# Attention and a gated feed-forward in one kernel: the constant of unseen keys from products on TensorE in place of pieces of ScalarE, and new ranks for the planner

## The chip, the core and the metric

The kernel runs on one core of a Trainium2 chip. The metric is device time in microseconds (us) of one execution. A core has five engines that run their own instruction queues beside each other and wait for one another by semaphores: TensorE (PE, products; PEld is its loading of weights), VectorE (DVE), ScalarE (ACT), GpSimd (POOL) and SyncE (SP, whose queue issues nearly all DMAs of this kernel). TensorE multiplies a stationary operand (up to 128 x 128) with a moving one and adds up in PSUM; the other engines read PSUM and work in SBUF.

## The reference

Block-causal attention (8 batches, 8 heads, 576 positions, 64 per head, blocks of 64), then a gated feed-forward on the 4608 rows of 512 that come out of it. The feed-forward's weights are 64-bit floats.

```python
scores = (1/sqrt(D)) * q @ k.T
mask   = (pos[:, None] // 64) >= (pos[None, :] // 64)
scores = where(mask, scores, -1e9)
attn   = exp(scores - max(scores)); attn /= sum(attn) + 1e-9
x      = (attn @ v) laid out as 4608 x 512
out    = (silu(x @ w_gate) * (x @ w_val)) @ w_out
```

## The kernel before

**Stages.** There is one program of some 7900 products, with no loop on the chip. Attention takes a batch's heads two at a time; the two heads sit in the two halves of 64 partitions (`own(x)`, x = 0 or 1), and their products stand in pairs. Keys are the partitions of the scores (chunks of 128, c = 0 to 4), queries the columns; a chunk needs only queries from c x 128 on. The first two batches (`early`) are cut into queries 0 to 255 and 256 to 575. Per pair of heads and stretch: transposes of q and k on PE (L410), ACT copies them out (L418, tile `parts`), scores on PE in plain float32 (L436, into the PSUM tiles `at` or `po`), ACT brings them to SBUF (L454, tile `sc`), DVE takes the maximum over chunks (L700, tile `mx`) and GpSimd over partitions (L704), DVE subtracts (L728), ACT takes the exponential (L732), and PE multiplies with the values and, in batch 0, with `ones` for the sums (L772). Batches 2 to 7 split q and k into high and low parts and take another path (`split_scores`, `row_scores`), which the change doesn't touch.

**The mask.** Only in a diagonal chunk, the one whose first query is c x 128, does the mask cut: its first 64 queries don't see its last 64 keys. So in the first 64 columns of such a chunk, partitions 64 to 127 need -1e9. Before, ACT adds it as a bias per partition (`unseen`: 0 in the upper half, -1e9 in the lower) in an operation of its own, after the plain copy: `hide` (L459, on 2 x 64 columns of one chunk), `hide_there` (L477, in PSUM itself, for batch 0's first 256 queries, whose scores stay in PSUM) and the second half of `first_max` (L468, beside a plain copy L467).

**Feed-forward.** 18 tiles of 256 rows. Per tile, six steps of two pieces of 128 hidden units: up products in reduced-width float32, three per 128 x 256 (high x high, high x low, low x high, L1095 to L1097, into two PSUM tiles `gv`), ACT's tanh (L1128), DVE's two gates (L1131, which also sets the gate's `gv` free, and L1136), ACT's high part (L1141), DVE's low part (L1144, `hhl`), and down products (L1186 to L1188, 128 x 512). Tiles 0 and 1 run in the first phase, their steps mixed in the order that `MIXED` gives.

**Weights.** 36 pieces of 512 KB are loaded into five raw buffers (tile `wo`) by SP (L939). Each is turned from 64-bit words into a high and a low part: ACT L954 and L958, DVE L963 and L968, ACT L973 (high) and DVE L976 (low). After L976 the raw buffer takes the next load.

**What sets the order.** Every piece of work is a `Task` with an engine, an estimated cost and a rank. `in_order` runs a model of the five engines while the kernel is built, gives an engine that is free the ready task of the lowest rank, and writes the tasks out in that order; nothing is decided on the chip. Ranks come from tables at the top: `PIECES` (weights, 12 x 3), `AHEAD` (their loads), `FIRST` (the two early batches, by stretch and pair of heads), `SIDE` (the feed-forward of tiles 0 and 1), `LEAD` and `EAGER` (later batches: rank 10 + b - LEAD), `spare` (how long an engine waits for a task of a better rank).

Of the kernel before, what the change touches and what calls it, by code (L numbers as in the profile page):

```python
# [18 lines left out]
def kernel(  # L19
# [17 lines left out]
    nc = tc.nc  # L37
# [15 lines left out]
    LEAD, EAGER = 1.69, 0.3  # L53
# [5 lines left out]
    MIXED = (0, 0, 1, 1, 0, 1, 0, 0, 1, 1, 0, 1)  # L59
# [3 lines left out]
    AHEAD = {(0, 1): 2.01, (0, 2): 2.07, (1, 0): 2.03, (1, 1): 2.5, (1, 2): 2.5}  # L63
    LATER = 0.6

    PIECES = [
        (2.46, 1.85, 2.03),
        (4.86, 5.95, 3.63),
        (4.60, 2.52, 1.48),
        (3.87, 3.06, 5.35),  # L70
        (1.93, 3.59, 2.41),
        (5.14, 6.91, 5.83),
        (3.58, 2.93, 2.93),
        (0.08, 1.36, 0.92),
        (-2.10, -5.86, -4.34),
        (-7.48, -5.87, -3.82),
        (-7.64, -9.14, -8.44),
        (-12.11, -9.50, -10.88),
    ]

    SIDE = (2.98, 4.19)
# [4 lines left out]
        0: [(0, 256, (-4.21, 2.41, 2.06, 2.12)), (256, 576, (-2.91, -2.07, -6.62, -4.11))],  # L86
        1: [(0, 256, (4.02, 3.94, 4.16, 3.63)), (256, 576, (-2.93, 1.90, 2.56, 4.50))],
# [97 lines left out]
    ones = const.tile([P, D], F32, name="ones")  # L185
# [4 lines left out]
    nc.vector.memset(unseen[BLK:P], HIDDEN)  # L190
    seen = const.tile([P, 1], F32, name="seen")
# [149 lines left out]
    def attention(R, b, h, a, e, early, bufs, lane):  # L341
# [4 lines left out]
        Q = R - (0.1 if early else EAGER)  # L346
# [30 lines left out]
        def plain_scores():  # L377
# [49 lines left out]
            for visit in visits:  # L427
                both = [Buf("at", also=banks) for _ in visit]

                def products(visit=visit, both=both):  # L430
                    for parts, ps in zip(visit, both):
                        o = 0
                        for c, qs, w in parts:
                            for x in range(2):
# [5 lines left out]
                                    start=True,  # L440
                                    stop=True,
# [3 lines left out]
                ws = [w for parts in visit for _, _, w in parts]  # L445
                pr = add("PE", pair_us(*ws), Q, products, ready, [*both, prt, sc], mode="rows")
                for parts, ps in zip(visit, both):
                    gw = sum(w for _, _, w in parts)
                    mixed = [(c, sum(w for _, _, w in parts[:i])) for i, (c, qs, _) in enumerate(parts) if qs == c * P]
# [6 lines left out]
                    def hide(mixed=mixed, ps=ps):  # L456

                        for c, o in mixed:
                            nc.scalar.activation(  # L459
                                sc[0][:, :, place[c] : place[c] + BLK],  # L460
                                ps[0][:, :, o : o + BLK],
                                AF.Identity,
                                bias=unseen,
                            )

                    def first_max(ps=ps):
                        nc.scalar.copy(mx[0][:, :, L + BLK : L + P], ps[0][:, :, BLK:P])  # L467
                        nc.scalar.activation(  # L468
                            mx[0][:, :, L : L + BLK], ps[0][:, :, 0:BLK], AF.Identity, bias=unseen
                        )  # L470

                    if whole:
                        stays.append(ps)

                        def hide_there(ps=ps):
                            x = ps[0].rearrange("p x (n w) -> p x n w", w=2 * P)[:, :, :, 0:BLK]
                            nc.scalar.activation(x, x, AF.Identity, bias=unseen)  # L477

                        def max_there(ps=ps):
                            nc.scalar.copy(mx[0][:, :, L : L + W], ps[0][:, :, 0:W])  # L480

                        t = add("ACT", act_us(4 * BLK) + 0.1, Q, hide_there, [pr], [ps])
                        t = add("ACT", act_us(2 * W), Q, max_there, [t], [ps, mx])
# [4 lines left out]
                    if mixed:  # L488
                        t = add("ACT", 0.245 * len(mixed), Q, hide, [t], [ps, sc])
                    if parts[0][:2] == (0, 0):  # L490
                        t = add("ACT", 0.46, Q, first_max, [t], [ps, mx])
# [791 lines left out]
    def in_order():  # L1283
# [14 lines left out]
        now = queue = 0.0  # L1298
        mode, last = "", None

        spare = {"PE": 2.12, "DVE": 0.32, "ACT": 0.75, "POOL": 0.0, "SP": 0.0}

        def place(t, by):

# [104 lines left out]
```

## Time and profile before

| | us |
|---|---|
| median of 3 runs | 1179.26 (1177.92 to 1181.79) |
| the profiled execution | 1177.14 |
| its span, first to last instruction | 1175.3 |
| PE busy from 0 to 200 us | 178.37 |
| DVE and ACT busy from 0 to 200 us | 167.18 and 158.44 |
| PE busy from 200 us to the end (975.3 us) | 970.65 |
| mean granted PE clock of the span | 0.994 |

Lines of the profile that the prediction reads are shown there. A group of a listing reads: line, engine, operation, output tile<-input tiles, shapes, count, then busy us and the mean ns of one, then the idle time of the engine just before such instructions and who ended it. In the trace a plain float32 product is two records. "gv L1095" in the waits and the chain stands for the tile that is written and the line that writes it.

### The profile page before, as it was taken

The numbers are of one execution on the slowest core, as the hardware profiler recorded it, in microseconds if no ns is written. First come the engines' busy times: TensorE is split into PE (matmuls) and PEld (weight loads), VectorE is DVE, ScalarE is ACT, GpSimd is POOL, SyncE is SP. The second block draws the span as 40 slices with busy tenths as digits, with TensorE's granted clock in tenths as the row PEclk, the third lists the DMA queues.
The fourth block names the chain that finished last, engine by engine and source line by source line (L and its number), as shares of the span: only waits on it lengthen the run. The fifth ranks groups of instructions, "written<-read, shape, count | busy, mean of one in ns | idle before, by whom it ended". The sixth has DMA issues, their size and how long they took to land.

```text
span 1175.3 us, 21803 instructions
## 1 busy us (share of the span) xinstructions
PE 1149.0 (98%) x8512; PEld 1026.9 (87%) x8512; DVE 754.4 (64%) x1226; ACT 625.0 (53%) x1122; POOL 323.7 (28%) x139
## 2 busy tenths in 40 slices
PE   6889999999999999999999999999999999999998
PEld 4568778898898989998999899899989899999997
DVE  5988988575887668768585867686857423323222
ACT  6889877546573837474656565656555212112111
POOL 3222100144535251335233433343324200000000
PEclk9899999999999999999999999999999999999999
DMA  8758756766554756755665565656553536453442
GB/s 213 200 150 217 197 187 227 209 177 166 170 145 139 198 165 167 218 148 158 177 173 153 155 175 146 191 157 173 151 182 125 160 136 190 145 168 135 144 132 102
DMA packets 266983, 197.40 MB, mean 168 GB/s; under 512 B 195264, under 2 KB 231376, under 8 KB 266880
## 3 DMA queue, kind: packets, MB, share of 16 engines
q1 hardware_dynamic: 264304, 195.29, 57.0%
q8 instruction: 67, 1.10, 0.4%
q10 hardware_dynamic: 2576, 0.72, 0.3%
q14 instruction: 36, 0.29, 0.1%
HBM read 171.57 MB, written 24.38 MB: 167 GB/s over the span
## 4 chain that ended last, share of the span: by engine, by line
PE 84%; DVE 6%; ACT 5%; DMA 2%; issue 1%; POOL 1%; SPq 1%; DVEq 0%; ACTq 0%; POOLq 0%
PE gv L1095 16%; PE gv L1097 15%; PE gv L1096 15%; PE po L1186 7%; PE po L1187 7%; PE po L1188 7%; PE at L772 7%; PE at L562 5%; DVE mx L700 1%; DMA wo<-in_moe_w_out_dram 1%; DVE sc L728 1%; PE po L772 1%; PE at L436 1%; ACT sc L732 1%; PE at L646 1%
## 5 line engine op out<-in xcount | busy, mean ns | idle before, releaser
L704 POOL PARTITION_ALL_REDUCE mx<-mx x80 | 142.9, 1833 | 400.4 <-DVE mx L700 126.3
L1095 PE MATMUL gv<-xhl,v_all 128*128 128x256 f32 x864 | 242.3, 280 | 0.8 <-DVE t L1131 0.7
L1097 PE MATMUL gv<-xhl,v_all 128*128 128x256 f32 x864 | 239.7, 277 | 0.2 <-DVE v_all L976 0.2
L1096 PE MATMUL gv<-xhl,v_all 128*128 128x256 f32 x864 | 239.5, 277 | 0.0
L823 POOL PARTITION_ALL_REDUCE mx<-mx x48 | 178.4, 3764 | 195.7 <-DVE mx L700 167.5
L1131 DVE SCALAR_TENSOR_TENSOR t<-t,gv 128x512 f32<-128x512 f32 x108 | 74.0, 685 | 190.4 <-ACT t L1128 190.2
L1095 PEld LDWEIGHTS gv<-xhl,v_all 128*128 128x128 f32 x864 | 162.1, 188 | 5.1 <-issue 2.5
L1096 PEld LDWEIGHTS gv<-xhl,v_all 128*128 128x128 f32 x864 | 162.3, 188 | 0.6
L1097 PEld LDWEIGHTS gv<-xhl,v_all 128*128 128x128 f32 x864 | 162.2, 188 | 0.4 <-DVE v_all L976 0.4
L1128 ACT ACTIVATE t<-gv 128x512 f32<-128x512 f32 x108 | 64.7, 599 | 173.4 <-PE gv L1097 173.3
L1186 PE MATMUL po<-wo,hhl 128*128 128x512 f32 x372 | 147.4, 396 | 0.2 <-ACT ob L1213 0.2
L1187 PE MATMUL po<-wo,hhl 128*128 128x512 f32 x372 | 145.7, 392 | 0.0
L1188 PE MATMUL po<-wo,hhl 128*128 128x512 f32 x372 | 145.1, 390 | 0.2 <-DVE hhl L1144 0.2
L1141 ACT CAST hhl<-t 128x512 fp32r<-128x512 f32 x108 | 67.1, 621 | 130.3 <-DVE t L1136 128.0
L732 ACT ACTIVATE sc<-sc 128x1024 f32<-128x1024 f32 (+3 forms) x104 | 105.9, 1031 | 52.2 <-DVE sc L728 51.5
L1136 DVE SCALAR_TENSOR_TENSOR t<-t,gv 128x512 f32<-128x512 f32 x108 | 73.8, 684 | 90.1 <-PE gv L1097 89.4
L728 DVE TENSOR_TENSOR sc<-sc,mx 128x640 f32<-128x640 f32 (+6 forms) x168 | 122.1, 766 | 13.9 <-POOL mx L704 13.8
L1095 PE MATMUL gv<-xhl,g_even 128*128 128x256 f32 x432 | 123.5, 286 | 0.0
L1097 PE MATMUL gv<-xhl,g_even 128*128 128x256 f32 x432 | 122.2, 283 | 0.0
L1096 PE MATMUL gv<-xhl,g_even 128*128 128x256 f32 x432 | 122.1, 283 | 0.0
L1095 PE MATMUL gv<-xhl,g_odd 128*128 128x256 f32 x432 | 120.8, 280 | 0.0
L1144 DVE TENSOR_TENSOR hhl<-t,hhl 128x512 fp32r<-128x512 f32 x108 | 91.2, 845 | 45.3 <-ACT hhl L1141 44.8
(172 smaller groups left out, 2445.4 us busy)
## 6 DMA issues: line engine op xcount, KB each, us to landing
wo<-wo_d SPq DMA_DIRECT2D x200, 512.0 KB
out_dram<-ob SPq DMA_DIRECT2D x35, 256.0 KB
v<-in_v_dram SPq DMA_DIRECT2D x64, 128.0 KB
xt<-x_d SPq DMA_DIRECT2D x64, 128.0 KB
rt<-r_d SPq DMA_DIRECT2D x128, 64.0 KB
qk<-in_q_dram SPq DMA_DIRECT2D x112, 72.0 KB
qk<-in_k_dram SPq DMA_DIRECT2D x104, 72.0 KB
x_d<-xu SPq DMA_DIRECT2D x24, 288.0 KB
```

What stands on the lines that cost most here:

```text
L704: nc.gpsimd.partition_all_reduce(m, m, channels=P, reduce_op=bass_isa.ReduceOp.max)
L728: nc.vector.tensor_tensor(piece(c), scores_of(c), m, ALU.subtract)
L732: nc.scalar.activation(x, x, AF.Exp)
L772: nc.tensor.matmul(ps[0][own(x), 1 - i if sums else i, q0 - s0 : s1 - s0], lhsT=ones if sums else vt[0][:, 2 * lane + c, own(x)], rhs=sc[0 ...
L823: nc.gpsimd.partition_all_reduce(m, m, channels=P, reduce_op=bass_isa.ReduceOp.add)
L1095: nc.tensor.matmul(o, lhsT=hi[:, d], rhs=xhi[:, 0:w], start=first, stop=False)
L1096: nc.tensor.matmul(o, lhsT=hi[:, d], rhs=xlo[:, 0:w], start=False, stop=False)
L1097: nc.tensor.matmul(o, lhsT=lo[:, d], rhs=xhi[:, 0:w], start=False, stop=last)
L1144: nc.vector.tensor_tensor(hh[1][:, 0:n], t[0][:, 0:n], hh[0][:, 0:n].bitcast(F32), ALU.subtract)
L1186: nc.tensor.matmul(po, lhsT=hi, rhs=whi, start=i + y == 0, stop=False)
L1187: nc.tensor.matmul(po, lhsT=hi, rhs=wlo, start=False, stop=False)
L1188: nc.tensor.matmul(po, lhsT=lo, rhs=whi, start=False, stop=i + y == NFC - 1)
```

## The change

The constant is added by PE, inside the scores' accumulation. A new tile `shade` has 64 columns of 0 and 64 of 1; a new column `hidden` is -1e9 in rows 0 and 64 and 0 elsewhere. After the scores of a diagonal chunk, one product for each head, stationary `shade` (64 rows x 128), moving `hidden` repeated over 64 columns, is added to the first 64 columns: 0 for the chunk's first 64 keys and -1e9 for the others. `hide`, `hide_there` and the second operation of `first_max` go; `first_max` becomes one plain copy. `ones` is now the second half of `shade`. The planner's tables get other numbers, `MIXED` swaps two steps, and early batches' first tasks (scores' evacuation, maxima) get the rank R - 1 in place of R - 0.1.

```diff
-    LEAD, EAGER = 1.69, 0.3
+    LEAD, EAGER = 1.32587, 0.3
-    MIXED = (0, 0, 1, 1, 0, 1, 0, 0, 1, 1, 0, 1)
+    MIXED = (0, 0, 1, 0, 1, 1, 0, 0, 1, 1, 0, 1)
...
-    ones = const.tile([P, D], F32, name="ones")
+    shade = const.tile([P, 2 * BLK], F32, name="shade")
+    nc.vector.memset(shade[:, 0:BLK], 0.0)
+    ones = shade[:, BLK : BLK + D]
     nc.vector.memset(ones, 1.0)
...
+    hidden = const.tile([P, 1], F32, name="hidden")
+    nc.vector.memset(hidden, 0.0)
+    for x in range(2):
+        nc.vector.memset(hidden[x * D : x * D + 1], HIDDEN)
...
-        Q = R - (0.1 if early else EAGER)
+        Q = R - (1 if early else EAGER)
...
                                     start=True,
-                                    stop=True,
+                                    stop=qs > c * P,
                                 )
+                            for x in range(2) if qs == c * P else ():
+                                nc.tensor.matmul(
+                                    ps[0][:, x, o : o + BLK],
+                                    lhsT=shade[own(x), :],
+                                    rhs=hidden[own(x), :].to_broadcast([D, BLK]),
+                                    start=False,
+                                    stop=True,
+                                )
...
-                    def hide(mixed=mixed, ps=ps):
-                        for c, o in mixed:
-                            nc.scalar.activation(
-                                sc[0][:, :, place[c] : place[c] + BLK],
-                                ps[0][:, :, o : o + BLK],
-                                AF.Identity,
-                                bias=unseen,
-                            )
                     def first_max(ps=ps):
-                        nc.scalar.copy(mx[0][:, :, L + BLK : L + P], ps[0][:, :, BLK:P])
-                        nc.scalar.activation(
-                            mx[0][:, :, L : L + BLK], ps[0][:, :, 0:BLK], AF.Identity, bias=unseen
-                        )
+                        nc.scalar.copy(mx[0][:, :, L : L + P], ps[0][:, :, 0:P])
...
-                        def hide_there(ps=ps):
-                            x = ps[0].rearrange("p x (n w) -> p x n w", w=2 * P)[:, :, :, 0:BLK]
-                            nc.scalar.activation(x, x, AF.Identity, bias=unseen)
...
-        spare = {"PE": 2.12, "DVE": 0.32, "ACT": 0.75, "POOL": 0.0, "SP": 0.0}
+        spare = {"PE": 2.3749, "DVE": 0.399612, "ACT": 0.379434, "POOL": 0.0, "SP": 0.0}
```

`PIECES`, `AHEAD`, `LATER`, `SIDE` and `FIRST` get new numbers in every place. What that moves is seen in the order of the built program. In its rows stand the line, the operation, output<-inputs with the buffers' numbers, and the shape; lines of the changed kernel are 8 higher up to the scores and 3 lower behind them.

At the very start of PE's program the first scores of batch 0 were, before:

```order
L410 MATMUL gv1_0_148<-ident_63,qk0_0_123 128x96 x3
L436 MATMUL at0_0_164<-parts0_0_155,parts0_1_156 128x256 x2
L436 MATMUL at0_0_164<-parts0_0_155,parts0_1_156 128x128 x2
L410 MATMUL gv0_0_142<-ident_63,qk0_0_123 128x96 x3
L410 MATMUL gv1_0_148<-ident_63,qk0_0_123 128x96 x3
```

and at the same place they now are:

```order
L418 MATMUL gv1_0_159<-ident_63,qk0_0_128 128x96 x3
L444 MATMUL at0_0_170<-parts0_0_163,parts0_1_164 128x256 x2
L453 MATMUL at0_0_170<-hidden_70,shade_64 128x64 x2
L444 MATMUL at0_0_170<-parts0_0_163,parts0_1_164 128x128 x2
L453 MATMUL at0_0_170<-hidden_70,shade_64 128x64 x2
L418 MATMUL gv0_0_155<-ident_63,qk0_0_128 128x96 x3
```

Behind the products of either diagonal chunk stands one more pair; the transposes around them stay.

On ACT, the same place in the program (the scores of the first two pairs of heads and the first weight) was, before:

```order
L418 ACTIVATE parts0_1_156<-gv1_0_148 128x288
L477 ACTIVATE at0_0_164<-at0_0_164,unseen_66 128x4x64
L480 COPY mx0_0_174<-at0_0_164 128x2x256
L418 ACTIVATE parts0_0_155<-gv0_0_142 128x288
L418 ACTIVATE parts0_1_156<-gv1_0_148 128x288
L418 ACTIVATE parts1_0_191<-gv0_0_142 128x288
L418 ACTIVATE parts1_1_192<-gv1_0_148 128x288
L954 ACTIVATE ob0_0_207<-wo0_0_94 128x512
L477 ACTIVATE at1_0_199<-at1_0_199,unseen_66 128x4x64
L958 ACTIVATE wo0_0_94<-wo0_0_94 128x512
L477 ACTIVATE po0_0_210<-po0_0_210,unseen_66 128x4x64
L480 COPY mx0_0_174<-at1_0_199 128x2x256
```

and is now:

```order
L426 ACTIVATE parts0_1_164<-gv1_0_159 128x288
L480 COPY mx0_0_181<-at0_0_170 128x2x256
L426 ACTIVATE parts0_0_163<-gv0_0_155 128x288
L426 ACTIVATE parts0_1_164<-gv1_0_159 128x288
L426 ACTIVATE parts1_0_203<-gv0_0_155 128x288
L426 ACTIVATE parts1_1_204<-gv1_0_159 128x288
L480 COPY mx0_0_181<-at1_0_207 128x2x256
L951 ACTIVATE ob0_0_233<-wo0_0_99 128x512
L729 ACTIVATE sc0_0_219<-sc0_0_219 128x2x384
L480 COPY mx1_0_251<-po0_0_221 128x2x256
```

The three L477 are gone, the second pair's copy to `mx` stands ahead of the first weight, and the weight's second step (L955) has moved behind the first exponential.

On DVE, late in the first phase, a raw buffer of weights that has been read out (L976, before) is read again after its next load (L963). Before, for raw buffer wo4:

```order
L976 TENSOR_TENSOR v_all1_74<-wo4_0_98,v_all0_73 128x4x128
L963 SCALAR_TENSOR_TENSOR wo1_0_95<-wo1_0_95,ob1_0_260 128x512
L700 TENSOR_TENSOR mx0_0_174<-mx0_0_174,sc0_0_215 128x2x192
L968 SCALAR_TENSOR_TENSOR wo1_0_95<-wo1_0_95 128x512
L700 TENSOR_TENSOR mx0_0_174<-mx0_0_174,sc0_0_215 128x2x64
L700 TENSOR_TENSOR mx1_0_241<-mx1_0_241,sc1_0_291 128x2x192
L700 TENSOR_TENSOR mx0_0_174<-mx0_0_174,sc0_0_215 128x2x320
L1131 SCALAR_TENSOR_TENSOR t0_0_609<-t0_0_609,gv0_0_142 128x512
L700 TENSOR_TENSOR mx1_0_241<-mx1_0_241,sc1_0_291 128x2x64
L1052 TENSOR_TENSOR xt0_0_271<-xt0_0_271,rt0_0_1577 128x256
L963 SCALAR_TENSOR_TENSOR wo4_0_98<-wo4_0_98,ob0_0_207 128x512
```

Now, for raw buffer wo0, twice (L973 and L960 are its lines now):

```order
L973 TENSOR_TENSOR wo1_0_1643<-wo0_0_99,wo1_0_1643 128x512
L1133 SCALAR_TENSOR_TENSOR t0_0_650<-t0_0_650,gv1_0_159 128x512
L1141 TENSOR_TENSOR hhl0_1_105<-t0_0_650,hhl0_0_104 128x512
L960 SCALAR_TENSOR_TENSOR wo0_0_99<-wo0_0_99,ob1_0_287 128x512
L965 SCALAR_TENSOR_TENSOR wo0_0_99<-wo0_0_99 128x512
L973 TENSOR_TENSOR v_all1_79<-wo0_0_99,v_all0_78 128x4x128
L960 SCALAR_TENSOR_TENSOR wo2_0_1693<-wo2_0_1693,ob0_0_233 128x512
L965 SCALAR_TENSOR_TENSOR wo2_0_1693<-wo2_0_1693 128x512
L697 TENSOR_TENSOR mx0_0_181<-sc0_0_219 128x2x320
L973 TENSOR_TENSOR wo4_0_1300<-wo2_0_1693,wo4_0_1300 128x512
L697 TENSOR_TENSOR mx0_0_181<-mx0_0_181,sc0_0_219 128x2x192
L960 SCALAR_TENSOR_TENSOR wo0_0_99<-wo0_0_99,ob1_0_287 128x512
```

Nine rows of other work stood between the two uses of wo4; two stand between the first two uses of wo0, and five between the next.

43 lines of the change are left out of this document (20 added, 23 removed).

## The prediction

> **What bounds the kernel now.** First the page: the span, and how much of it TensorE (PE) is busy.
>
> ```profile
> span 1175.3 us, 21803 instructions
> PE 1149.0 (98%) x8512; PEld 1026.9 (87%) x8512; DVE 754.4 (64%) x1226; ACT 625.0 (53%) x1122; POOL 323.7 (28%) x139
> ```
>
> PE leaves 26 us of 1175.3 open, so the time is PE's own work plus those gaps. Where they lie is told by the busy times by stretch: start and end, its length, then busy us (and instructions) of PE, weight loads, VectorE (DVE), ScalarE (ACT) and GpSimd (POOL), then the granted PE clock and the DMA share.
>
> ```profile
> 0.00:20.00 20.00, 12.39 (x73) 9.62 (x74) 7.91 (x28) 11.19 (x23) 8.82 (x16) 0.93 0.85 210
> 20.00:50.00 30.00, 22.67 (x172) 14.60 (x172) 28.24 (x58) 26.59 (x48) 7.62 (x6) 0.88 0.76 204
> 50.00:80.00 30.00, 26.69 (x222) 19.48 (x219) 26.59 (x53) 23.69 (x49) 5.95 (x5) 0.94 0.57 154
> 80.00:130.00 50.00, 49.69 (x388) 39.96 (x387) 44.77 (x80) 45.54 (x93) 12.45 (x10) 1.00 0.76 209
> 130.00:160.00 30.00, 26.93 (x189) 20.42 (x187) 25.14 (x46) 22.27 (x40) 2.76 (x2) 1.00 0.69 201
> 158.50:1175.30 1016.80, 1012.15 (x7489) 923.77 (x7489) 623.29 (x970) 495.90 (x874) 286.13 (x101) 1.00 0.55 164
> ```
>
> Up to 160 us PE is open for 7.6 + 7.3 + 3.3 + 0.3 + 3.1 = 21.6 us; from 158.5 on for 4.65 us in all, most of it behind the last product. So only the first 160 us can give anything, and there DVE (28.2 of 30 from 20 to 50 us) and ACT (26.6 of 30) are both nearly full. The waits of PE in the first 200 us (who waited for whom, us, times, longest) name both:
>
> ```profile
> PE at L436 <- ACT sc L459: 3.1, 2, 1.6
> PE at L772 <- ACT sc L459: 2.4, 2, 1.2
> PE gv L1095 <- DVE t L1131: 0.7, 1, 0.7
> ```
>
> L459, one of the operations that the change removes, ends 5.5 us of PE's waits in these two rows. The last wait before PE runs through is the 0.7 us for DVE's L1131 (start, us, group, idle before it):
>
> ```profile
> 158.50 0.39 PE L1095 MATMUL gv<-xhl,v_all 128*128 128x256 f32 x1 [0.71 <-DVE t L1131]
> ```
>
> **How I count.** What the whole first phase costs is one number: how far PE stands behind its own work at its last wait. I add up PE's work ahead of that matmul, in program order, at full clock, with prices from these rows of the timeline (scores L436 and values L772) and of the chain (the up and down products):
>
> ```profile
> 127.55 1.13 PE L436 MATMUL at<-parts,parts 64*128 64x320 f32 x8
> 128.62 0.39 PE L1095 MATMUL gv<-xhl,g_odd 128*128 128x256 f32 x1
> ...
> 131.99 0.98 PE L436 MATMUL at<-parts,parts 64*128 64x320 f32 x8
> 132.89 0.39 PE L1095 MATMUL gv<-xhl,v_all 128*128 128x256 f32 x1
> ...
> 135.55 0.81 PE L436 MATMUL at<-parts,parts 64*128 64x320 f32 x4
> 136.29 0.38 PE L1095 MATMUL gv<-xhl,v_all 128*128 128x256 f32 x1
> ...
> 151.43 2.27 PE L772 MATMUL at<-sc,v 128*64 128x320 f32 x20
> ```
>
> ```profile
> 159.12 0.12 PE gv L1095
> 172.16 0.23 PE po L1187
> ```
>
> An up product is 0.117, a down product 0.234. A pair of score products (one per head) of 320 columns takes 0.74 to the next group, 320 + 64 take 0.90, 320 + 192 take 1.07: 0.2 for the change of kind and 0.05 + 0.0015 per column for a pair. A pair of value products is 0.03 + columns/600 (ten pairs, 2.2), a transpose 0.083, a change of kind 0.1 to 0.2. Ahead of the matmul at 158.50 stand 309 up products (36.2), 60 down (14.1), 118 transposes (9.8), 51 pairs of scores (19.9), 83 pairs of values (32.7) and 11.2 for changes: 123.8. PE is **34.7 us behind its work**: gaps, half-clock time and start together.
>
> DVE I count alike, each row of its order at the mean of its group (257 rows ahead of and with that L1131; two of its groups, with 27 and 7 of them):
>
> ```profile
> L968 DVE SCALAR_TENSOR_TENSOR wo<-wo 128x512 int32<-128x512 int32 x35 | 25.1, 721 | 1.6 <-ACT wo L958 1.3
> L1131 DVE SCALAR_TENSOR_TENSOR t<-t,gv 128x512 f32<-128x512 f32 x10 | 6.8, 682 | 1.3 <-ACT t L1128 1.3
> ```
>
> The sum is 145.8, so DVE is 12.6 behind at 158.4. Its lag is made at the start and then hardly grows: 110.1 of work stand ahead of and with the first row here, which ends at 121.3, a lag of 11.2; with the second it is 177.7 at 193.3, a lag of 15.6.
>
> ```profile
> 120.66 0.68 DVE L1131 SCALAR_TENSOR_TENSOR t<-t,gv 128x512 f32<-128x512 f32 x1
> ...
> 192.66 0.68 DVE L1144 TENSOR_TENSOR hhl<-t,hhl 128x512 fp32r<-128x512 f32 x1
> ```
>
> So 34.7 = 22.0 (DVE's work less PE's work at that wait) + 12.6 (DVE's lag).
>
> **Part by part. The products.** 40 diagonal chunks (2 batches, 4 pairs of heads, 2 + 3 chunks) get 2 products of 64 columns each, of the form that L436 has already. From 0.74 to 0.90 one such pair costs 0.16: 40 x 0.16 = **+6.4 us** of PE work. Bounds: columns alone, (1.07 - 0.90)/128 x 64 = 0.085 a pair, give 3.4; the duration of one record of this form, taken as if nothing overlapped (160 records), gives 13.4. I stay with the difference of two rows, which is the thing itself.
>
> ```profile
> L436 PE MATMUL at<-parts,parts 64*128 64x64 f32 x32 | 2.7, 244 | 0.0
> ```
>
> The difference between 0.085 and 0.16 is a fixed part of 0.075 a pair. The Trainium skill (TensorEngine Tiling (Array Packing), Instruction Overhead) speaks against such products: each matmul carries an overhead of about 60 cycles, so that a free size of 1 takes as long as one of 60. By that rule 64 columns cost as 124, 40 x 0.085 x 124/64 = 6.6 us, an estimate from that page; without it 3.4. The trace agrees with the page here.
>
> **ACT's operations go.**
>
> ```profile
> L459 ACT ACTIVATE sc<-at,unseen 128x128 f32<-128x128 f32 x28 | 10.0, 374 | 0.1
> L477 ACT ACTIVATE at<-at,unseen 128x256 f32<-128x256 f32 x3 | 1.3, 441 | 1.8 <-PE at L436 1.8
> L468 ACT ACTIVATE mx<-at,unseen 128x128 f32<-128x128 f32 x3 | 1.2, 403 | 0.0
> L787 ACT COPY xu<-at 128x256 f32<-128x256 f32 x4 | 1.5, 383 | 0.2 <-PE at L772 0.2
> ```
>
> 32 L459 (with the four that read the other buffer, 12.0), four L477 (1.7), and the two-piece first maximum (0.40 + 0.29, four times) against one copy like L787's (0.38, four times), 1.2: about 14.9 us of ACT in the first 185 us. ACT's work less PE's at PE's waits on ACT counted in the same way, falls from at most 29.7 to 16.0. With a lag of about 8.8 (what ACT leaves open of the first 20 us), ACT then holds PE at 25, below what DVE holds (next), so nothing of these 14.9 us comes through directly: DVE is late next. On the first chain L477's 0.45 goes and two pairs of products at half clock, about 0.6, come.
>
> **Ranks.** DVE's work is the same but for three small memsets. What moves is how much of it stands ahead of PE's steps. The largest difference at a PE wait in the new order is at the third L1131 (now L1128): 217 DVE rows, 114.1 us, and PE's 97.5 (21.1 up, 8.4 down, 9.8 transposes, 15.8 scores, 4.5 of the new products, 29.3 values, 8.6 changes): 16.5 against 22.0. Other waits from 70 to 126 us of PE work have 11 to 15; after that it falls to 6 to 10. With the lag of 10.5 to 11.2 that DVE has at that depth: **27.5 us behind**, bounds 26.0 (lag 9.5, were the start 1.5 shorter) and 29.1 (lag 12.6). That gives back 34.7 - 27.5 = 7.2.
>
> **The raw buffers.** Late in the phase weights wait for a raw buffer to be read out; from the chain (start, us, what), freed by DVE at 148.08, the next load's first DVE step is at 154.68:
>
> ```profile
> 147.47 0.61 DVE g_even L976
> 148.10 5.74 DMA wo<-in_moe_w_out_dram
> 153.86 0.80 ACT ob L954
> 154.68 0.69 DVE wo L963
> ```
>
> Such a turn takes 6.6. In the new order DVE has 1.4 us of rows between freeing wo0 and reading it again (146 us into its work), then 3.4 for the turn after: 5.2 and 3.2 of stall, and 1.0 at one before with 5.6 of rows. The same reckoning for the order before gives 10 where DVE's lag grew by 4.4 from 11.2 to 15.6. At 175.1 of PE's work DVE has 184.9 ahead: 9.8 plus a lag of 15.1 to 20.3 makes 25 to 30: it may tie with 27.5, and I leave it there.
>
> **LEAD** (1.69 to 1.33) starts the later batches' attention 0.36 of a batch later. I cost it at nothing: from 158.5 us on PE's gaps are 4.65 us, and DVE and ACT are busy 61% and 49% of that stretch; were that cover gone, a batch that comes late would stop PE outright.
>
> **The sum.** 1175.3 + 6.4 - 7.2 = 1174.5 of span. The profiled execution took 1177.14, 1.84 over its span, and the median of the runs, 1179.26, is 2.1 over that: **1178.4**.
>
> **Rivals.** *Faster.* The pieces of ACT were holding DVE too, and a part of the new products lies in gaps that PE has anyway: columns alone (3.4) and 26.0 behind give 1175.3 + 3.4 - 8.7 = 1170.0, so 1173.9. For it: L459 ends 5.5 us of PE's waits, and DVE waits for ACT here and there (1.3 us in L968's row). Against it: the difference of rows says 0.16, and DVE is full from 20 to 50 us. Chance 0.31.
>
> *Slower.* The raw buffer is the bound: where a turn takes 7.1 each time (half a us over the one above) and nothing overlaps, four reuses with 1.4, 3.4, 5.6 and 5.7 of rows between stall DVE for 5.7 + 3.7 + 1.5 + 1.4 = 12.3, its lag at 175 of PE's work is 11 + 12.3 = 23.3, PE is 33.1 behind, and 1175.3 + 6.4 - 1.6 = 1180.1, so 1184.2. It decides from a lag of 17.7 on (27.5 - 9.8); from 24.9 on nothing is won and the products are paid in full. For it: 1.4 us of rows against a turn of 6.6. Against it: the same count overstates the order before by more than double. Chance 0.15.
>
> *The clock.* From 40 to 50 us it was 0.66 (the share behind the five engines), though the rows of the waits show none there over 1.6 us:
>
> ```profile
> 40.00:50.00 10.00, 8.74 (x50) 5.04 (x52) 9.06 (x17) 8.21 (x16) 2.38 (x2) 0.66 0.78 206
> ```
>
> That stretch lost 3.4 us of PE's clock. In the new order PE follows DVE closely from 70 to 126 us of its work, with many short waits; if they halve the clock once more behind the last wait, 3.4 come on top: 1181.8. Chance 0.04. The Trainium skill (TensorE: Matmul & The Clock Gate, HAM oscillation) asks for an idle gap over about 3.4 us before the clock falls; by that rule it would not fall here at all, but the trace has it fall after shorter ones, and the measurement decides.
>
> **How the numbers follow.** The forecast has 0.50, its own range 1176 to 1181. About 0.3% (3.5 us) is what a measurement of this kernel can tell from no change. Faster by more: the first rival, nearly whole, and the forecast's low edge, 0.32. Slower by more: the raw buffer, and a little of the clock and of the products' upper bound, 0.18. Within: 0.50. The range takes in most of the rivals on both sides: 1172.5 to 1184.5.
>
> **What would show it.** Right: about 160 new records on PE, adding 6 to 7 us of its work; no wait of PE on ACT's score pieces; DVE as full as before up to 130 us; PE's last wait earlier in its work (near 100 to 126 instead of 124), at a distance of about 27 to 28 behind. Wrong: PE's open time in 0 to 160 us much below 14 us, or its last waits in 140 to 175 us on what a late load feeds, or waits behind 200 us, which LEAD would make.

## The result and the profile after

The changed kernel takes **1185.47 us** (median of 8 runs, 1182.91 to 1188.97), the kernel before 1178.57 on the same chips (8 runs, 1177.55 to 1181.79). The ratio is 1.0058, interval [1.0047, 1.0069]: slower by 5.5 to 8.1 us, where 1178.4 was forecast, in a range of 1172.5 to 1184.5. The profiled execution took 1182.91, the fastest of the eight; its span is 5.8 us longer than that of before.

The first two lines of the changed kernel's page, to be read beside those of before that the prediction quotes:

```profile
span 1181.1 us, 22067 instructions
PE 1155.3 (98%) x8672; PEld 1036.9 (88%) x8672; DVE 769.2 (65%) x1230; ACT 611.7 (52%) x1082; POOL 323.2 (27%) x139
```

PE has 160 records more and is busy 6.3 us longer. Its open time, span less busy time, is 25.8 us against 26.3. So by this account the span grew by the products' whole length, and the gaps out of which they were to be paid are as large as before. (It is an account and not yet a cause: with the products shortened, below, the time stayed.) The busy times by stretch show that the gaps moved. Columns as in the prediction; three stretches of the kernel before:

```profile
0.00:80.00 80.00, 61.75 (x460) 43.70 (x461) 62.74 (x138) 61.47 (x119) 22.39 (x26) 0.91 0.71 187
80.00:200.00 120.00, 116.62 (x859) 94.94 (x858) 104.44 (x178) 96.97 (x180) 20.89 (x17) 1.00 0.70 211
200.00:600.00 400.00, 399.18 (x2999) 361.22 (x2999) 287.11 (x449) 236.49 (x418) 152.07 (x52) 1.00 0.61 170
```

and of the changed kernel:

```profile
0.00:80.00 80.00, 65.44 (x556) 49.95 (x556) 60.88 (x139) 57.25 (x104) 22.57 (x26) 0.94 0.78 186
80.00:200.00 120.00, 116.19 (x896) 96.17 (x895) 103.38 (x177) 87.31 (x148) 21.50 (x17) 1.00 0.71 203
200.00:600.00 400.00, 396.19 (x2976) 357.37 (x2975) 284.26 (x434) 226.16 (x399) 143.16 (x49) 1.00 0.61 169
```

PE is open for 80 - 65.44 = 14.6 us up to 80 us, 3.7 less than before. From 80 to 200 it is 3.8 (3.4 before), and from 200 to 600 it is 3.8, where there were 0.8. What was won at the start is lost again behind 200 us. Who is waited for there, by the waits of the changed kernel up to 320 us (us in total, times, longest):

```profile
PE at L769 <- DVE xt L803: 3.2, 1, 3.2
PE at L444 <- ACT parts L426: 2.6, 2, 1.5
PE at L418 <- ACT parts L426: 1.9, 2, 1.2
...
PE po L1183 <- ACT ob L1210: 1.4, 1, 1.4
PE at L1185 <- DVE hhl L1141: 1.3, 1, 1.3
```

No wait on ACT's score pieces is left. The last two rows are waits at 308 and 208 us. In the timeline of the changed kernel the single waits on ACT's and DVE's steps behind 75 us stand in brackets:

```profile
81.08 0.55 PE L418 MATMUL at<-ident,qk 96*128 96x96 f32 x4 [1.01 <-DVE xt L803]
82.86 0.71 PE L418 MATMUL at<-ident,qk 96*128 96x96 f32 x6 [1.23 <-ACT parts L426]
...
166.11 1.13 PE L444 MATMUL at<-parts,parts 64*128 64x320 f32 x8 [0.77 <-ACT sr L845]
...
208.33 0.50 PE L1185 MATMUL at<-wo,hhl 128*128 128x512 f32 x1 [1.27 <-DVE hhl L1141]
...
308.01 0.50 PE L1183 MATMUL po<-wo,hhl 128*128 128x512 f32 x1 [1.38 <-ACT ob L1210]
```

They are many small waits at different places, not one. Weights come into some of them. On the chain of the changed kernel two loads into raw buffers stand late in the phase, each ahead of one of these waits (166 and 208 us):

```profile
158.22 6.02 DMA wo<-in_moe_w_val_dram
...
194.74 5.06 DMA wo<-in_moe_w_val_dram
```

and between 20 and 320 us ACT waits 14.4 us for weights,

```profile
ACT ob L951 <- DMA wo<-in_moe_w_val_dram: 6.5, 4, 3.4
ACT ob L951 <- DMA wo<-in_moe_w_out_dram: 4.0, 3, 2.9
ACT ob L951 <- DMA wo<-in_moe_w_gate_dram: 3.9, 3, 2.3
```

where the kernel before has 5.4:

```profile
ACT ob L954 <- DMA wo<-in_moe_w_out_dram: 3.8, 2, 2.3
ACT ob L954 <- DMA wo<-in_moe_w_val_dram: 1.6, 2, 1.1
```

Such waits don't cost time by themselves. The order of before with the new mask (an experiment below, 1180.59 us) has 11.1 us of them:

```profile
ACT ob L959 <- DMA wo<-in_moe_w_out_dram: 5.6, 4, 2.0
ACT ob L959 <- DMA wo<-in_moe_w_val_dram: 3.2, 4, 1.8
ACT ob L959 <- DMA wo<-in_moe_w_gate_dram: 2.3, 3, 1.5
```

### The profile page after: what moved, and what is told of

It reads as the page before. It is cut to its first block, busy times and chain, and to the rows that moved or that the text cites. A ratio compares the mean times of both kernels' runs of the same rounds, so it can differ in the third digit from the quotient of the medians.

```text
span 1181.1 us, 22067 instructions
## 1 busy us (share of the span) xinstructions
PE 1155.3 (98%) x8672; PEld 1036.9 (88%) x8672; DVE 769.2 (65%) x1230; ACT 611.7 (52%) x1082; POOL 323.2 (27%) x139
## 4 chain that ended last, share of the span: by engine, by line
PE 87%; DVE 5%; ACT 3%; DMA 2%; issue 1%; POOL 1%; DVEq 0%; SPq 0%; ACTq 0%; POOLq 0%
PE gv L1092 16%; PE gv L1093 16%; PE gv L1094 16%; PE po L1183 7%; PE po L1184 7%; PE po L1185 7%; PE at L769 7%; PE at L559 6%; PE at L444 1%; DVE mx L697 1%; DMA wo<-in_moe_w_val_dram 1%; PE at L643 1%; DVE sc L725 1%; POOL mx L701 1%; PE at L1185 1%
## 5 line engine op out<-in xcount | busy, mean ns | idle before, releaser
L1128 DVE SCALAR_TENSOR_TENSOR t<-t,gv 128x512 f32<-128x512 f32 x108 | 73.7, 682 | 157.4 <-ACT t L1125 156.9
L1183 PE MATMUL po<-wo,hhl 128*128 128x512 f32 x372 | 147.5, 397 | 1.4 <-ACT ob L1210 1.4
L1185 PE MATMUL po<-wo,hhl 128*128 128x512 f32 x372 | 145.4, 391 | 0.0
L1141 DVE TENSOR_TENSOR hhl<-t,hhl 128x512 fp32r<-128x512 f32 x108 | 100.7, 932 | 35.2 <-ACT hhl L1138 34.9
```

The lines of the kernel that those rows point to most:

```text
L1141: nc.vector.tensor_tensor(hh[1][:, 0:n], t[0][:, 0:n], hh[0][:, 0:n].bitcast(F32), ALU.subtract)
L1183: nc.tensor.matmul(po, lhsT=hi, rhs=whi, start=i + y == 0, stop=False)
L1185: nc.tensor.matmul(po, lhsT=lo, rhs=whi, start=False, stop=i + y == NFC - 1)
```

## The experiments

A ratio is the kernel's time over that of before, run beside it on the same chip, five rounds each; 0.001 is 1.2 us. "Open" is PE's open time from 0 to 80, 80 to 200 and 200 to 600 us in the profiled execution, worked out from the stretches as above.

| | median us | ratio, interval | open us |
|---|---|---|---|
| before | 1178.6 to 1180.2 | 1 | 18.3, 3.4, 0.8 |
| changed | 1185.47 | 1.0058 [1.0047, 1.0069] | 14.6, 3.8, 3.8 |
| new order, old mask | 1192.86 | 1.0116 [1.0103, 1.0129] | 18.3, 9.7, 3.9 |
| old order, new mask | 1180.59 | 1.0013 [1.0003, 1.0023] | 15.0, 1.5, 1.2 |
| old order, no mask | 1177.64 | 0.9989 [0.9978, 1.0000] | 16.6, 2.7, 2.1 |
| old order, both masks | 1182.47 | 1.0032 [1.0020, 1.0044] | 16.4, 3.0, 0.6 |
| old order, short products | 1178.94 | 0.9999 [0.9990, 1.0008] | 16.5, 2.3, 1.1 |
| new order, short products | 1186.52 | 1.0060 [1.0047, 1.0073] | 17.9, 3.8, 4.8 |
| new order, products twice | 1194.48 | 1.0127 [1.0113, 1.0140] | 13.2, 4.0, 3.8 |
| new order, table early | 1185.42 | 1.0048 [1.0035, 1.0061] | 13.1, 4.7, 3.7 |
| LEAD back | 1188.55 | 1.0082 [1.0064, 1.0100] | 18.2, 4.9, 4.1 |
| first batches' ranks back | 1211.65 | 1.0284 [1.0265, 1.0303] | 16.5, 8.3, 22.0 |
| weights' ranks back | 1192.27 | 1.0135 [1.0102, 1.0169] | 20.8, 3.4, 1.7 |
| all ranks back, planned anew | 1206.88 | 1.0229 [1.0205, 1.0254] | 18.6, 10.0, 6.7 |
| new order, loads cut | 1180.87 | 1.0017 [1.0007, 1.0027] | 14.6, 2.5, 2.8 |
| old order, loads cut | 1174.84 | 0.9969 [0.9959, 0.9979] | 18.9, 0.1, 1.2 |
| old order, new mask, loads cut | 1179.65 | 0.9991 [0.9980, 1.0002] | 15.3, 0.6, 0.7 |
| new order, less DVE | 1185.42 | 1.0053 [1.0039, 1.0067] | 16.3, 3.6, 3.0 |
| old order, less DVE | 1178.44 | 1.0002 [0.9992, 1.0011] | 19.1, 2.9, 1.2 |
| new order, copies first | 1185.47 | 1.0062 [1.0044, 1.0080] | 14.7, 3.1, 1.9 |

### The order and the mask apart

Two parts of the change were separated: the written-out order and the mask. The changed kernel's order with the mask as before:

```diff
-                            for x in range(2) if qs == c * P else ():
-                                nc.tensor.matmul(
-                                    ps[0][:, x, o : o + BLK],
-                                    lhsT=shade[own(x), :],
...
                         nc.scalar.copy(sc[0][:, :, o : o + gw], ps[0][:, :, 0:gw])
+                        for i, (c, qs, _) in enumerate(parts):
+                            if qs == c * P:
...
+                                    AF.Identity,
+                                    bias=unseen,
```

> The changed kernel's written-out order, with the mask as before: ScalarE adds the constant in pieces after the copy, and the 160 new records on PE are gone; nothing else differs. The changed kernel takes 1185.5 us, the kernel before 1178.6. Theory A (the order): the products lie in time that PE waits for VectorE anyway, and the new order loses by its own late waits (at 138 to 166, 200 to 240 and 308 us) and its later start: then this kernel stays near the changed one, 1184 to 1187. Theory B (the products): PE has no room for them, 40 pairs by 0.16 us are paid in full, and the order alone is worth what it was: then 1178 to 1180.

and the order of before with the new products, `hide`, `hide_there` and the second half of `first_max` emptied:

> The order of the kernel before, with the constant from products of 64 rows on PE and without ScalarE's pieces (some 15 us of ScalarE less); nothing else differs. Theory A (the order): the products lie in PE's 21.6 us of open time up to 160 us, and ScalarE's relief can only help: 1174 to 1179. Theory B (the products): paid in full, 1178.6 + 6.4 = 1185, less what ScalarE's relief gives (5.5 us of PE's waits ended on its pieces), so 1182 to 1185.

Measured: 1192.86 and 1180.59. The second lies just above what A gave and below what B gave: in the order of before the whole change of the mask is nearly free. The first lies 5.9 us above all that either theory allowed: I had taken ScalarE's relief for small in any order. PE's busy time in it from 80 to 200 us, then that of the old order with the new mask:

```profile
80.00:200.00 120.00, 110.33 (x790) 88.36 (x790) 98.73 (x171) 93.02 (x170) 17.73 (x14) 0.96 0.65 186
```

```profile
80.00:200.00 120.00, 118.55 (x931) 98.40 (x930) 104.24 (x177) 92.06 (x154) 21.57 (x18) 1.00 0.72 206
```

9.7 us are open against 1.5. Gaps aren't the whole of it. The page of the new order with the old mask reads

```profile
PE 1154.8 (97%) x8512; PEld 1029.8 (86%) x8512; DVE 770.8 (65%) x1230; ACT 624.5 (52%) x1122; POOL 322.1 (27%) x139
```

so PE takes 5.8 us longer for the same 8512 records than in the kernel before, and the granted clock is 0.990 in each of its four runs, against 0.994 to 0.998 in the changed kernel. ScalarE's pieces also stand in an order here that was planned without them.

So the mask's change costs 1.5 us in the old order and saves 6.8 in the new one (1.0116 to 1.0058), and the new order costs 13.7 us with the old mask and 5.3 with the new. The new order is the loss, with either mask. (The new order without any mask wasn't run, so what the products alone cost in it isn't known.)

### The parts of the mask, in the order of before

Neither part (the mask left out), then both (ScalarE's pieces kept, products added):

> The order of before with neither ScalarE's pieces nor the new products: the mask of the first two batches is left out. This is ScalarE's relief of some 15 us by itself. The prediction's step (ScalarE isn't what holds PE, nothing of it comes through): 1178 to 1179, as before. Rival (ScalarE's relief is worth the 4.8 us by which PE's gaps fell in the order of before with the new products, from 22.6 to 17.8): 1173.5 to 1175.

> The order of before with ScalarE's pieces kept and the new products added (the constant is added twice, which changes no result). This is the products by themselves. The prediction's step (products ahead of a wait for VectorE take no time, since VectorE's work sets that wait): 1178.5 to 1181. Rival (paid in full, 40 pairs by 0.16 us): 1184.5 to 1186.

1177.64 and 1182.47. ScalarE's relief alone gives 1.3 us, at most 2.6, not 4.8: the prediction's step is nearly right and the rival falls. The products alone cost 3.8 us [2.4, 5.2], between the two: of their 6.3 us on PE some two fifths lie in waits.

### The length of the products

In bfloat16 in place of float32, in either order:

```diff
-    hidden = const.tile([P, 1], F32, name="hidden")
+    shade16 = const.tile([P, P], mybir.dt.bfloat16, name="shade16")
+    hidden = const.tile([P, 1], mybir.dt.bfloat16, name="hidden")
-                                    lhsT=shade[own(x), :],
+                                    lhsT=shade16[own(x), :],
```

> The order of before with the new products in bfloat16 in place of float32 (0 and -1e9 rounded to bfloat16, which changes no result), so one pass and one record for a product instead of two; no ScalarE pieces. If the products are paid on PE: some 0.05 to 0.08 us a pair instead of 0.17, so 3.5 to 4.8 less than with float32 (1180.6): 1175.8 to 1177, which beats both kernels. If PE's waits hide them: 1180 to 1181, as with float32.

> The changed kernel (order and all) with the new products in bfloat16 in place of float32. If the products are paid on PE in the new order (doubling them cost 9.0): 3.5 to 4.8 less than 1185.4, so 1180.6 to 1182. If waits hide them: 1185.

and the products of the changed kernel issued twice:

```diff
-                            for x in range(2) if qs == c * P else ():
+                            for y in range(2) if qs == c * P else ():
+                                for x in range(2):
-                                    stop=True,
+                                        stop=y == 1,
```

> The changed kernel with every new product issued twice (80 pairs instead of 40; the constant becomes -2e9, which changes no result). Theory B (products paid in full, 0.16 us a pair): 40 more pairs, +6.4, so 1191 to 1192.5. Theory A (they lie in PE's waits for VectorE): +0 to +2.5, 1185 to 1188. The trace also gives the price of a pair by itself: 0.16 by the prediction, 0.085 if only columns count.

In the trace of the second a short pair takes 0.03 us to the next product (76.07 to 76.10), where a float32 pair takes 0.17, so some 5.6 us of PE's work are gone with 40 pairs. The fixed part of 0.075 us a pair in the prediction is therefore one of float32 products and not of every product. In the old order the short products save 1.7 us (1.0013 to 0.9999), less than half of what was expected. In the new order they save nothing: PE's busy time falls from 1155.3 to

```profile
PE 1152.1 (97%) x8592; PEld 1028.2 (87%) x8592; DVE 768.0 (65%) x1231; ACT 611.5 (52%) x1082; POOL 323.7 (27%) x139
```

and its open time up to 600 us grows from 22.2 to 26.5. Up to 83 us PE's waits end some 2 us earlier than in the changed kernel, but from 166 us on they end at the same times: 166.29, 208.48 and 308.13 us here, 166.11, 208.33 and 308.01 there. What ends them there is not PE's own work. Doubled, the products cost 8.1 us more by the ratios (1.0127 against 1.0058), above the 6.4 of B. In the timeline of that kernel two pairs take 0.40 us at full speed (84.08 to 84.48), where one pair takes 0.17 in the changed kernel (78.18 to 78.35), so 0.23 for the second pair, 9.2 for 40:

```profile
84.08 0.56 PE L454 MATMUL at<-hidden,shade 64*128 64x64 f32 x8
84.48 0.44 PE L444 MATMUL at<-parts,parts 64*128 64x128 f32 x4
```

```profile
78.18 0.34 PE L453 MATMUL at<-hidden,shade 64*128 64x64 f32 x4
78.35 0.44 PE L444 MATMUL at<-parts,parts 64*128 64x128 f32 x4
```

So in the new order shorter products are worth nothing, and more of them are paid nearly in full (8.1 of 9.2 us).

### The start

```diff
+    order.remove(table)
+    order.insert(next(i for i, t in enumerate(order) if t.engine == "ACT") + 1, table)
```

> The changed kernel with ScalarE's load of its table of functions moved in the written-out order from behind the eight DMA issues on its queue to behind the first of them (it stood at 6.18 us, before at 1.73; the first copy of ScalarE began at 7.58, before at 5.43). If the later start passes through to the end (part of theory A), 1 to 2 us less: 1183.5 to 1184.5. If later waits take it up again, 1185 to 1186, the same as the changed kernel.

The median is 1185.42, the same; the ratio is 1.2 us lower than the changed kernel's (1.0048 against 1.0058), and the intervals can't tell that from nothing. The open time up to 80 us falls by 1.5 us, and 0.9 of it comes back from 80 to 200. PE's first product starts at 5.56 us here and at 5.64 in the changed kernel, behind a load of q, where it starts at 3.96 before: this part of the later start was not moved.

### Groups of ranks put back

One group of tables at a time was put back in the changed kernel and the order planned anew: LEAD; `FIRST` and R - 0.1; `PIECES`, `AHEAD`, `LATER`, `SIDE` and `MIXED`; then all, `spare` with them.

> The changed kernel with LEAD back at 1.69, planned anew; all other numbers as changed. The changed kernel takes 1185.4 us; the order of before with the new products takes 1180.6, so the new ranks lose 4.9, of which 2.8 us are PE's gaps behind 200 us (1.8 at 200 to 250, 1.0 at 308; the order of before has 0.6 and 0). Theory L (LEAD makes the waits behind 200 us): 1181.5 to 1183.5. Theory W (the weights' ranks make them, since they hang on a weight's turn) or theory F (the first batches' ranks are the loss): 1184.5 to 1187.

> The changed kernel with the ranks of the first two batches as before (the FIRST table, and R - 0.1 in place of R - 1), planned anew. Theory F (these ranks lose by the later start, 1.2 us more of gaps up to 10 us, and by what they push behind at 80 to 100 us, 2.3 more): 1181 to 1184. Theory W or L: 1184.5 to 1188, since the tables were set for one another.

> The changed kernel with the ranks of the weights and of the first feed-forward tiles as before (PIECES, AHEAD, LATER, SIDE, MIXED), planned anew. Theory W (weights that come late stop PE at 80 to 100 and 200 to 250 us, 4.1 us of gaps more than in the order of before): 1181 to 1183.5. Theory F or L: 1184.5 to 1188.

> The new products and no ScalarE pieces, with every table of numbers as before, planned anew (unlike the earlier run, which kept the order of before as it was written out). If what loses is the new ranks: like that run, 1179 to 1182. If the tables of before fit only the tasks that they were set for: 1183 to 1190.

All are slower than the changed kernel, by 2.8 us (LEAD; 0.3 to 5.3 by the intervals), 26.6, 9.1 and 20.2, so none of the three theories gets the gain that it expected, and the last lies above both of its ranges. With LEAD back the same waits behind 200 us stand there, the one at L1185 in this row of its timeline:

```profile
211.02 0.50 PE L1185 MATMUL at<-wo,hhl 128*128 128x512 f32 x1 [1.27 <-DVE hhl L1141]
```

so LEAD alone doesn't make them. With the weights' ranks back neither this wait nor the one at 308 us stands there, and PE's open time from 200 to 600 us is 1.7; but that execution took 1204.41 us, 12 more than its median, at a granted clock of 0.944, and a slower PE may wait less, so this is a hint and no proof. With the first batches' or all ranks back there are other and longer gaps in this stretch (22.0 and 6.7). Which group makes the loss can't be read from these runs. Even the tables of before, planned with tasks that they weren't found for, lose 27 us, where the order of before, kept as it was written out, loses 1.5.

### What PE waits for: VectorE's work or the weights' loads

```diff
-                m = mx[0][:, :, L + first[c] - a : L + W]
-                nc.vector.tensor_tensor(piece(c), scores_of(c), m, ALU.subtract)
+                o = 0 if stays or not early else e - first[c] - BLK
+                m = mx[0][:, :, L + first[c] - a + o : L + W]
+                nc.vector.tensor_tensor(piece(c, o), scores_of(c, o), m, ALU.subtract)
```

> The changed kernel with VectorE's 48 subtractions of the maximum in the first two batches (0.65 us each) cut to the last 64 queries of each stretch (for the others the maximum isn't subtracted, which leaves the quotients as they are for scores of this size): some 20 us of VectorE less up to 190 us; order and all else as changed. Theory V (VectorE's work sets PE's waits): most of PE's 11 us of gaps between 20 and 310 us go, 1176 to 1181. Theory R (raw buffers' turns set them): 1184 to 1185.5.

> The kernel before with the same cut of VectorE's subtractions. The prediction's step (VectorE's work and lag make the 34.7 us by which PE stands behind its work): PE's gaps of 14 us between 20 and 160 us go for the most part, 1168 to 1173. If ScalarE takes VectorE's place (it ended 5.5 us of PE's waits): 1173 to 1177.

```diff
+            if 3 * i + kind in (*range(5, 29), 30, 33):
+                n, m = (1, 2 * P) if kind < 2 else (1, DM // 2)
+                view, src = view[:, 0:n, 0:m], src[:, 0:n, 0:m]
             nc.sync.dma_start(out=view, in_=src)
```

> The changed kernel with 26 of the 31 weight loads that reuse a raw buffer cut to a quarter of their bytes (the rest of the buffer keeps what it had, so the feed-forward computes with wrong weights); order and all else as changed. Theory R (the new order waits for raw buffers' turns: weight loads of 6.0 and 5.1 us stand on its chain at 158 and 195 us, and ScalarE waits 14.4 us for weights, against 5.4 in the kernel before): 2 to 4 us less than 1185.5, 1181.5 to 1183.5. Theory V (VectorE's own work and its late start set PE's waits): 1184.5 to 1186.

> The kernel before with the same 26 weight loads cut to a quarter of their bytes. Theory R: the order of before has one such turn on its chain, behind its last wait but one, so 0 to 2 us less than 1179: 1177 to 1179. Theory V: 1178 to 1179.

The cut of VectorE's work (the first two of these four) came out at 14.7 us in the new order (769.2 to 754.5 on the pages) and 11.8 in the old (754.4 to 742.6), not 20. Neither kernel is faster by a measurable amount (1.0053 against 1.0058, 1.0002 against 1). Theory V falls in both orders. The loads give 4.8 us in the new order and 3.7 in the old; in the old order PE's gaps from 80 to 200 us all but vanish, from 3.4 to 0.1:

```profile
80.00:200.00 120.00, 119.89 (x891) 97.73 (x891) 107.77 (x185) 100.31 (x184) 20.88 (x17) 1.00 0.53 152
```

Theory R holds for both orders alike, and more for the old one than I had expected.

In the changed kernel with the loads cut the waits at 166 and 208 us are gone, and small ones on the gate step have come; those from 77 to 83 us and the one at 308 stand as they were. Three rows of its waits up to 320 us (308 us, 81 us, and the new ones; L1186, L1213 and L1131 are L1183, L1210 and L1128 of the changed kernel):

```profile
PE po L1186 <- ACT ob L1213: 1.4, 1, 1.4
PE at L418 <- DVE xt L803: 1.0, 1, 1.0
PE gv L1095 <- DVE t L1131: 0.8, 3, 0.4
```

So late loads make the waits at 166 and 208 us, as the chain had them. At 208 VectorE has a share: with its work cut, 0.31 of the 1.27 us is left there. What about the loads counts is not separated: shorter loads end a raw buffer's turn earlier, and they also take traffic off the DMA engines, whose share from 80 to 200 us falls from 0.71 to 0.54.

The next run asks whether theory R makes the difference of the two orders. It is the old order with the new products and the loads cut:

> The order of before with the new products (no ScalarE pieces) and the same 26 weight loads cut to a quarter of their bytes (wrong weights in the feed-forward). Set against the changed kernel with the same cut, 1180.9 us. If the weights' turns are what the new order loses by (4.9 us with whole loads): the two orders meet, 1180 to 1182. If the weights hold both orders alike and the new order loses elsewhere: 1180.6 less the 4.2 to 4.6 of either order, 1176 to 1176.5.

1179.65 (0.9991), between the two: with the loads cut the new order is still slower by 1.0017 - 0.9991, 3.1 us, against 5.3 with whole loads. The loads may explain 2 us of the difference (the intervals leave 0 to some 5); the rest lies elsewhere.

### One place on ScalarE's queue

In the changed kernel two copies (`ob`, L1210), whose products had ended at 305.1 us, stood on ACT's queue behind an exponential that waited for DVE (start, us, then what; idle time in brackets):

```profile
305.83 1.17 ACT L729 ACTIVATE sc<-sc 128x1152 f32<-128x1152 f32 x1 [2.00 <-DVE sc L725]
306.90 1.06 ACT L1210 COPY ob<-po 128x512 f32<-128x512 f32 x2
```

```diff
+    order.remove(ahead)                                   # this L729
+    order.insert(order.index(ends_of[5]) + 1, ahead)      # behind the two copies
```

> The changed kernel with one exponential of ScalarE moved: at 305.8 us it waited 2.0 us for VectorE, and the two copies that empty tile 1's sums stood behind it on ScalarE's queue, though their products had ended at about 305.1; they now stand ahead of it. In the changed kernel PE's next down product then waits 1.38 us for these copies (1.37 to 1.38 in every run of the new order but the one with the weights' ranks back). Theory Q (the new ranks put work that isn't ready ahead of copies that PE waits for): PE's wait at 308 falls below 0.5 us, its open time from 200 to 600 us from 3.8 to 2.7, and the time by 1.0 to 1.4 us, to 1184 to 1184.5. If another work then ends late: the wait goes and comes back behind it, 1185.5.

In the profile they have changed places, PE's wait at 308 is gone, and its open time from 200 to 600 us falls from 3.8 to 1.9:

```profile
304.28 1.08 ACT L1210 COPY ob<-po 128x512 f32<-128x512 f32 x2 [1.43 <-PE po L1185]
305.38 1.18 ACT L729 ACTIVATE sc<-sc 128x1152 f32<-128x1152 f32 x1
```

```profile
200.00:600.00 400.00, 398.06 (x2991) 359.47 (x2990) 287.05 (x436) 226.03 (x401) 145.13 (x50) 1.00 0.61 170
```

The profiled span is 1179.1, 2.0 less. (Of the replanned kernels, those with the first batches' or all ranks back hadn't this wait either; the expectation leaves them out.) The median of six runs, 1185.47 with an interval of 4.2 us, can't tell 1.4 us from nothing, and it lies above the 1184 to 1184.5 expected: shown is that this wait comes from the place of one exponential ahead of two copies, not what it is worth in the median.

No run beats the kernel before with the whole computation; the nearest is the old order with short products, equal to it. What the mask's change could give in the old order at most is the run without any mask, 1.3 us (0 to 2.6).

## Why the prediction was wrong, step by step

**The step that failed** is the count of DVE's rows: that PE's 34.7 us behind its work are "22.0 (DVE's work less PE's work at that wait) + 12.6 (DVE's lag)", and that an order with 16.5 in place of 22.0 "gives back 34.7 - 27.5 = 7.2". The numbers add up, but they aren't a cause: such a sum holds whatever PE waits for. With 12 to 15 us of DVE's work taken out the time stayed, in either order; with the loads shortened it fell by 3.7 and 4.8. Of the 7.2 us, 0.5 is left at the end (PE's open time of 25.8 us against 26.3). At the wait that I had named (97.5 us of PE's work ahead of it; it is the fourth L1128 in the trace, not the third, as the prediction miscounted) the chain of the changed kernel reads

```profile
126.66 0.69 DVE t L1128
127.39 0.39 PE gv L1092
```

and 127.4 less the 97.5 of PE's work is 29.9: from there to 160 us PE has no gap, so 4.8 of the 7.2 were there at 160 us, and by 320 us they were gone again.

**The products** are sized rightly as work (6.4 forecast; 160 records, 6.3 us by the page, 6.8 by the 0.17 us of a pair in the timeline). The sum took them as paid in full. In the old order 3.8 us of them reach the end. In the new one the page's account has them all, but with some 5.6 us of them taken out the time stayed, so there they aren't what sets it.

**ScalarE's 14.9 us.** That "nothing of these 14.9 us comes through directly" holds in the old order (1.3 us). For the new order it fails: with the pieces put back that order loses 6.8 us, though the products are gone from PE, partly by longer gaps and partly by a slower PE (9.7 us more of gaps up to 600 us than in the changed kernel, and 5.8 us more for the same records than in the kernel before).

**The raw buffers.** The words "it may tie with 27.5, and I leave it there" left out what the runs show to count. Of the three cuts tried in both orders (the products' length, VectorE's work, the loads) only that of the loads helped clearly in both. The slower rival named this place and gave 1184.2 (its terms add up to 1184.0); that its time is near is luck in good part, for its mechanism explains at most part of it, since shortened loads help the old order nearly as much.

**LEAD at nothing** isn't refuted (with LEAD back the kernel is 2.8 us slower, and the waits behind 200 us stay), but the sum also took for granted that PE runs through behind 158.5 us. That was a property of the old order, not of the stage: the new order adds 3.0 us of gaps from 200 to 600.

**The signs** that were to show it right: the 160 records came, the waits on the score pieces went, and DVE was as full up to 130 us (99.5 us from 20 to 130, against 99.6). The fourth didn't: PE's last waits don't lie near 100 to 126 us of its work, but at 166, 208 and 308 us. Two of the three signs that were to show it wrong came, the wait at 166 us on what a late load feeds and waits behind 200 us. The other, an open time up to 160 us much below 14, did not: it was 17.6, where the sum wanted 14.4.

**What stays open:** which of the new ranks makes the waits from 77 to 83 us, and what makes the 3.1 us by which the new order is slower with the loads cut too. DVE's amount of work, LEAD alone and the loads are excluded as makers of the waits from 77 to 83; those at 166 and 208 us come with the loads, and the one at 308 us with a place on ACT's queue. `spare` was not put back by itself.

## What to carry to other kernels

A sum of two engines' work up to a wait always balances; to make it a cause, take work off the engine and see whether the wait moves. A profile without gaps in a stage tells of the order that ran, so a new order has to be priced for all stages, the quiet ones too. Ranks that were found for one set of tasks did not carry over to another here, whole or in part; the old order kept as it was written out did, at 1.5 us.

## What the runs showed of the hardware

PE's first products run at about half speed although the granted clock (the last column but two) stands at 1.00 there, and how long that lasts differs between kernels. In the changed kernel four records of 256 columns take 1.23 us at 13 us and 0.70 at 20 (from their start to that of the next group 1.01 and 0.51):

```profile
0.00:20.00 20.00, 11.82 (x84) 9.97 (x84) 7.16 (x30) 8.74 (x18) 7.51 (x15) 1.00 0.81 174
```

```profile
13.05 1.23 PE L444 MATMUL at<-parts,parts 64*128 64x256 f32 x4
...
19.94 0.70 PE L444 MATMUL at<-parts,parts 64*128 64x256 f32 x4 [0.38 <-DVE sc L725]
```

With the products twice they still take 1.22 at 23.5 us, 18 us after the first product:

```profile
23.54 1.22 PE L444 MATMUL at<-parts,parts 64*128 64x256 f32 x4
```

The kernel with the early table has the same products as the changed one and the same open time up to 600 us within 0.7 (21.5 and 22.2), yet PE is busy 1160.0 us against 1155.3:

```profile
PE 1160.0 (98%) x8672; PEld 1040.3 (88%) x8672; DVE 768.6 (65%) x1230; ACT 611.9 (52%) x1082; POOL 323.8 (27%) x139
```

4.7 us between two profiled executions are the speed of PE alone, so one profile of each can't decide between orders that differ by less. The Trainium skill (TensorE: Matmul & The Clock Gate, Part 1: The HAM clock gate) has the array start at half rate and be freed after one busy window of about 3.4 us, whose phase runs free. The half rate at the start agrees with these rows; the 18 us of it, with no gap of PE above 1.5 us between and none in the rows from 8.14 to 21.7 us, don't.
